# A planner's cost table, a split of each visit's last products, and three transfers in flight instead of five, in a retention + PReLU MLP kernel

## The chip, the cores and the metric

One core of a Trainium2 chip runs the whole program. The metric is device time in microseconds; lower is better. A measurement of this kernel tells about 0.3% from no change.

## The reference

Two stages in float32. The first is a retention layer: for each of 8 batches and 8 heads, `scores = q k^T / 8` over 576 positions of 64 numbers, multiplied by a lower triangle of decays `gamma_h ** (i - j)`, then times `v`. The result is turned to 4608 tokens by 512 channels. The second is an MLP:

```
h = x @ w_in                                   # 4608x512 by 512x2048
g = np.maximum(h, 0.0) + alpha * np.minimum(h, 0.0)
out = g @ w_out                                # 4608x2048 by 2048x512
```

## The kernel before, in words

**The MLP.** The tokens are cut into 18 blocks of 256, d_ff into 8 units of 256. A *cell* is one block with one unit: its first product (L1057, 48 matmuls of 256 columns in two halves) goes to the PSUM banks psh0 and psh1, ACT and DVE turn it into `ga` (L1064 to L1071), ACT and POOL split it into three pieces `g` (L1080 to L1087), and its second product (L1105, 12 matmuls of 512 columns, six for each half m of the tokens) adds to four banks pso. Both operands are split in pieces of a short float type ("fp32r"), so that three cheap products replace a slow float32 one. A *visit* is a block with four units (or all eight); at its end `evacuate` (L1116 to L1133) combines, for each m, two banks: first the bank p1 of the cross products (a subtraction on DVE, L1123, or a copy on ACT), then p0 (DVE, L1128), and a DMA takes the result to HBM. The first eight cells are done in plain float32 while weights are still being prepared (`unit_plain` L992, `second_plain` L1023).

**Retention.** Batches 0 and 1 are done early in parts (`load_part`, `part_transposes` L447, `part_scale` L423 on POOL, `part_scores` L471, `part_states` L493, `part_values` L540 and L556, `last_part`). Batches 2 to 7 are 24 pairs of heads, each one call of `joint` among the MLP cells: float32 matmuls of 64 columns that make scores and states ("su", L867 and L870, with two more matmuls "x", L860) of one pair and the values of the pair before ("v0" and "v1", L808, in the banks psh that the first products use too).

**The order.** Nothing is issued while this is described: `do` records each piece of work with an engine, a cost in us, a function, and what it reads and writes. `plan` first walks backwards for a due time of each piece, then forwards: at each step, on each engine, it takes the pieces that could begin within SLACK of the earliest one, and of these the one due first. SWITCH is added to a piece's earliest start if its *kind* differs from the last piece on that engine. The costs only choose the order of issue; on the chip each engine runs its own list in order, held up by semaphores. Before the change SLACK is 0.14 us and SWITCH 0.12 us on PE; only "su" pieces have a kind of their own ("half"), so the planner sees no difference between a value product and an MLP product.

**Transfers.** Nearly all DMAs are issued by one queue, SP's, in order (L220); the first two loads of q are issued by ACT. While the planned time is below LIMITED (100 us), a DMA on SP gets one more wait: going back over the DMAs planned before it, it adds their bytes to its own, and where the sum has reached IN_FLIGHT, it waits for the landing of the next older one. With 5 << 18 bytes that is the fifth DMA back for loads of 256 KiB. What stands behind a waiting DMA on SP waits too. In order, the early loads are: q, k of the first half of the first part, the same of the second half, v twice, four loads of w_in, two of w_out of 512 KiB, then the next parts and weights.

Of the kernel before, what the change touches and what calls it, by code (L numbers as in the profile page):

```python
# [21 lines left out]
def kernel(  # L22
# [58 lines left out]
    def piece(x):  # L81
        return x.bitcast(PIECE)
# [148 lines left out]
        do(eng, 0.56, f, r, w, late=size / rate, hold=hold)  # L231

    flight, now = [], [0.0]
    LIMITED, IN_FLIGHT = 100.0, 5 << 18

    LAT = {"PE": 0.2}

# [100 lines left out]
    BACKLOG, HOLD = 2.0, 30.0  # L338
    LAG, HOLD_X = 2, 100.0
    GROUPS = (("v0",), ("v1",), ("x", "su"))  # L340
    SLACK, SWITCH = {"PE": 0.14}, {"PE": 0.12}
    BEGIN = {"PE": 5.0, "ACT": 0.5, "DVE": 8.2, "POOL": 5.8, "SP": 0.5}


# [488 lines left out]
    def on_pe(parts, groups):  # L833
        for some in groups:
            do("PE", sum(parts[x][0] for x in some), lambda some=some: [parts[x][1]() for x in some],
               [key for x in some for key in parts[x][2]],
               [key for x in some for key in parts[x][3]],
               kind="half" if "su" in some else None)

    def joint(n):  # L840
        pv = [Gen(psh[m]) for m in range(2)]
        parts = {}
        if n - 1 in mts:
            (parts["v0"], parts["v1"]), rest = values(n - 1, pv)
        if n == len(pairs):
            on_pe(parts, [["v0"], ["v1"]])
            rest()
            return
        c = pairs[n][1]
        kT, qT = turned[n]  # L850
        kn, vn = loaded[n][2:]

        ss, uu = (Gen(x) for x in psa)

        def chunks(x):
            return x.get().rearrange("p (j s) -> p j s", s=C)

        def f():
            for h2 in range(2):
                nc.tensor.matmul(pv[1].get()[half(h2), 7 * C:], kT.get()[half(h2), chunk(NJ - 1)],  # L860
                                 qT.get()[half(h2), chunk(NJ - 1)], start=True, stop=True)
        parts["x"] = 0.067, f, [(kT, 0), (qT, 0)], [(pv[1], "x")]

        def f():
            for j in range(NJ - 1):
                for h2 in range(2):
                    nc.tensor.matmul(chunks(ss)[half(h2), j], kT.get()[half(h2), chunk(j)],  # L867
                                     qT.get()[half(h2), chunk(j)], start=True, stop=True,
                                     skip_group_check=True)
                    nc.tensor.matmul(chunks(uu)[half(h2), j], kn.get()[half(1 - h2), j],  # L870
                                     vns[n % 2][half(1 - h2), h2, j], start=True, stop=True,
                                     skip_group_check=True)
        parts["su"] = (1.05, f, [(kT, 0), (qT, 0), (kn, 0), (kn, 1), (vn, "v", 0), (vn, "v", 1)],
                       [(ss, 0), (uu, 0), (uu, 1)])
        on_pe(parts, [some for some in ([x for x in group if x in parts] for group in GROUPS)
                      if some])
        if n - 1 in mts:
            rest()
            if n + 1 < len(pairs):
                load_v(n + 1)  # L880
        mt = mts[n] = Gen(ats)
        for h2 in range(2):
            to = lambda h2=h2: mt.get()[half(h2), h2].rearrange("p j s -> p (j s)")
            dma(to, lambda h2=h2: qT.get()[half(h2)], S * D * 4, [(qT, 0)], [(mt, "q", h2)])

        def masked(h2, j, fro):
            x, h = half(h2), 2 * c + h2
            nc.vector.scalar_tensor_tensor(  # L888
                out=mt.get()[half(1 - h2), h2, j], in0=fro[x], scalar=pf[x, 1, h:h + 1],
                in1=mask[x, None, :].to_broadcast([C, fro.shape[1], C]), op0=ALU.mult,  # L890
                op1=ALU.mult)
        for h2 in range(2):
            do("DVE", 0.69, lambda h2=h2: masked(h2, slice(0, NJ - 1), chunks(ss)), [(ss, 0)],
               [(mt, "s", h2)])
        for h2 in range(2):
            do("DVE", 0.285, lambda h2=h2: masked(h2, slice(NJ - 1, NJ), chunks(pv[1])[:, 7:]),
               [(pv[1], "x")], [(mt, "x", h2)])
        su = Gen(sus)
        g1, g2 = gch[:, 0, c:c + 1], gch[:, 1, c:c + 1]
        do("ACT", 0.37, lambda: nc.scalar.copy(su.get()[:, 0::2], chunks(uu)[:, 0::2]), [(uu, 0)],  # L900
           [(su, "e")])
        do("DVE", 0.45, lambda: nc.vector.scalar_tensor_tensor(
            out=chunks(uu)[:, 1::2], in0=su.get()[:, 0::2], scalar=g1, in1=chunks(uu)[:, 1::2],
            op0=ALU.mult, op1=ALU.add), [(su, "e")], [(uu, 1)])
        do("ACT", 0.22, lambda: nc.scalar.copy(su.get()[:, 1], chunks(uu)[:, 1]), [(uu, 1)],
           [(su, 1)])
        for j in range(3, NJ - 1, 2):
            do("DVE", 0.285, lambda j=j: nc.vector.scalar_tensor_tensor(
                out=su.get()[:, j], in0=su.get()[:, j - 2], scalar=g2, in1=chunks(uu)[:, j],
                op0=ALU.mult, op1=ALU.add), [(su, j - 2), (uu, 1)], [(su, j)])  # L910
        do("DVE", 0.42, lambda: nc.vector.scalar_tensor_tensor(
            out=su.get()[:, 2::2], in0=su.get()[:, 1:NJ - 3:2], scalar=g1,
            in1=chunks(uu)[:, 2::2], op0=ALU.mult, op1=ALU.add),
            [(su, 1), (su, 3), (su, 5), (uu, 0)], [(su, "e")])
        for h2 in range(2):
            to = lambda h2=h2: vns[n % 2][half(h2), h2, 1:]
            keys = [(su, x) for x in ("e", 1, 3, 5, 7)]
            dma(to, lambda h2=h2: su.get()[half(h2)], (S - C) * D * 4, keys, [(vn, "s", h2)])
# [123 lines left out]
    def unit(cell):  # L1042
# [3 lines left out]
        for f in range(2):  # L1046
            ph = Gen(psh[f])

            def at(b, ph=ph):
                return ph.get()[:, b * TB:(b + 1) * TB]  # L1050

            def mm(f=f, at=at):
                for n, (b, l) in enumerate(((0, 0), (1, 2), (0, 1))):
                    for cc in range(NCC):
                        w = w_piece(u, cc // 2, l)
                        c0 = (cc % 2 * 2 + f) * P
                        nc.tensor.matmul(at(b), w[:, c0:c0 + P],  # L1057
                                         piece(x.get()[:, l, cc]), start=(n == 0 and cc == 0),
                                         stop=(n > 0 and cc == NCC - 1), skip_group_check=True)
            do("PE", 1.43, mm, [(x, l, n) for l in range(3) for n in range(2)] +  # L1060
               [w_at[u, i][l] for i in range(2) for l in range(3)], [(ph, 0), (ph, 1)])
            fc = 2 * u + f
            g = lambda f=f: ga.get()[:, f]
            do("ACT", 0.36, lambda g=g, at=at: nc.scalar.copy(g(), at(1)), [(ph, 1)], [(ga, f)])  # L1064
            do("DVE", 0.42, lambda g=g, at=at: nc.vector.scalar_tensor_tensor(  # L1065
                out=g(), in0=at(0), scalar=ONE, in1=g(), op0=ALU.mult, op1=ALU.subtract),
                [(ph, 0)], [(ga, f)])
            do("ACT", 0.39, lambda g=g, at=at: nc.scalar.activation(at(1), g(), ACTF.Relu,  # L1068
                                                                    scale=-1.0),
               [(ga, f)], [(ph, 1)])  # L1070
            do("DVE", 0.48, lambda g=g, at=at, fc=fc: nc.vector.scalar_tensor_tensor(  # L1071
                out=g(), in0=at(1), scalar=malpha[:, fc:fc + 1], in1=g(), op0=ALU.mult,
                op1=ALU.add), [(ph, 1), (cst, "a")], [(ga, f)])
# [19 lines left out]
    def second(cell):  # L1093
# [5 lines left out]
                dma(lambda: vis["o"].get(), lambda: o_kept[vis["kb"]], P * 4096,  # L1099
                    [(okm[vis["kb"]], 0), (okm[vis["kb"]], 1)], [(vis["o"], 0), (vis["o"], 1)])  # L1100
        for m in range(2):
            def mm(m=m, a=list(acc)):
                for f in range(2):
                    for b, l in ((0, 0), (0, 1), (1, 2)):
                        nc.tensor.matmul(a[2 * m + b].get(),  # L1105
                                         piece(g.get()[:, l, f, m * P:(m + 1) * P]),
                                         w_piece(u, 2 + f, l),
                                         start=(cell["first"] and f == 0 and l != 1),
                                         stop=(cell["last"] and f == 1 and l > 0))
            do("PE", 1.375, mm, [(g, l) for l in range(3)] +  # L1110
               [w_at[u, i][l] for i in (2, 3) for l in range(3)],
               [(acc[2 * m], 0), (acc[2 * m + 1], 0)])
            if cell["last"]:
                evacuate(vis, m)

# [248 lines left out]
```

## Time and profile before

| | |
|---|---|
| median of 3 runs | 954.3 us (952.51 to 955.4) |
| the profiled execution | 958.57 us |
| its span, first to last instruction | 956.5 us |
| around the span (difference) | 2.07 us |
| PE busy / DVE / ACT / POOL | 930.8 / 554.1 / 573.8 / 576.8 us |
| mean granted TensorE clock | 0.994 |
| DMA bytes | 121.05 MB, mean 127 GB/s |

PE is TensorE's matmuls, PEld its weight loads, DVE is VectorE, ACT ScalarE, POOL GpSimd, SP the queue engine. A row of the waits tells who waited for whom; a row of a timeline begins with its start and its length in us. In a timeline the lengths of neighbouring groups on PE overlap, since matmuls are pipelined, so a group's cost is read from its start to the start of the next.

### The profile page before, as it was taken

The page shows a single profiled execution, that of the slowest core. Times are in us where ns is not written, and L with a number is a line of the kernel's source. Part 1 is how long each engine was busy: PE and PEld are TensorE (multiplying, and loading weights), DVE is VectorE, ACT ScalarE, POOL GpSimd, SP SyncE. Part 2 cuts the span into 40 slices and gives each one's busy share as a digit, 9 for nine tenths or more (in the row PEclk, how much of TensorE's full clock was granted, in tenths as well). Part 3 has the DMA queues.
Part 4 walks back from the last instruction along what each step waited for, and adds up shares of the span by engine and source line. Part 5 has one row for each costly group of instructions (what it writes and reads, how often), then busy time and mean ns, then how long its engine had stood idle before and what let it go on. Part 6 is the DMA issues. An engine that isn't in the chain of part 4 may idle for free.

```text
span 956.5 us, 22974 instructions
## 1 busy us (share of the span) xinstructions
PE 930.8 (97%) x9009; PEld 820.8 (86%) x9009; DVE 554.1 (58%) x1180; ACT 573.8 (60%) x1285; POOL 576.8 (60%) x473
## 2 busy tenths in 40 slices
PE   4899999999999999999999999999999999999998
PEld 4666689888988898888999999999999999999996
DVE  5668566665766676766665754544444554444444
ACT  3446556657667666657876775555555555555542
POOL 3557765748865668745775565555555555555543
PEclk9899999999999999999999999999999999999999
DMA  8867587777877877785434411122222111121212
GB/s 213 203 178 149 134 182 170 151 173 166 186 181 179 199 178 171 209 174 147 155 121 144 156 54 45 67 78 78 86 88 70 67 67 66 66 67 68 66 45 66
DMA packets 235532, 121.05 MB, mean 127 GB/s; under 512 B 203408, under 2 KB 203424, under 8 KB 235424
## 3 DMA queue, kind: packets, MB, share of 16 engines
q1 hardware_dynamic: 233312, 119.05, 47.4%
q8 instruction: 71, 1.16, 0.5%
q10 hardware_dynamic: 2112, 0.53, 0.3%
q14 instruction: 37, 0.30, 0.1%
HBM read 74.19 MB, written 31.98 MB: 111 GB/s over the span
## 4 chain that ended last, share of the span: by engine, by line
PE 91%; DVE 2%; POOL 2%; ACT 2%; issue 1%; DMA 1%; ACTq 0%; POOLq 0%; DVEq 0%
PE psh L1057 40%; PE pso L1105 39%; PE psh L808 3%; PE pso L1023 2%; PE psh L992 2%; PE psa L870 2%; DMA w<-in_q_dram 1%; PE psh L860 1%; PE psa L867 1%; POOL w L732 1%; ACT x L571 1%; DVE psa L679 0%; POOL w L423 0%; ACT w L669 0%; POOL lx L975 0%
## 5 line engine op out<-in xcount | busy, mean ns | idle before, releaser
L1057 PEld LDWEIGHTS psh<-lx,w 128*128 128x128 f32 x2832 | 356.3, 191 | 11.6 <-DVE ga L1071 0.6
L1057 PE MATMUL psh<-lx,w 128*128 128x256 f32 x2832 | 364.2, 284 | 0.0
L1105 PE MATMUL pso<-w,g 128*128 128x512 f32 x1416 | 350.0, 393 | 1.4 <-DVE o L1128 1.2
L1084 POOL TENSOR_TENSOR g<-ga,g 128x512 fp32r<-128x512 f32 x136 | 175.8, 1293 | 243.4 <-ACT g L1080 217.8
L1105 PEld LDWEIGHTS pso<-w,g 128*128 128x128 f32 x1416 | 256.5, 189 | 50.0 <-DVE o L1128 1.4
L1065 DVE SCALAR_TENSOR_TENSOR ga<-psh,ga 128x256 f32<-128x256 f32 x272 | 115.0, 423 | 192.8 <-ACT ga L1064 189.3
L1087 POOL TENSOR_TENSOR g<-g 128x512 fp32r<-128x512 f32 x136 | 176.0, 1294 | 11.7 <-ACT g L1082 1.5
L1064 ACT COPY ga<-psh 128x256 f32<-128x256 f32 x272 | 101.3, 373 | 134.7 <-PE psh L1057 118.4
L1071 DVE SCALAR_TENSOR_TENSOR ga<-psh,malpha,ga 128x256 f32<-128x256 f32 x272 | 130.7, 481 | 69.5 <-ACT psh L1068 68.6
L1068 ACT ACTIVATE psh<-ga 128x256 f32<-128x256 f32 x272 | 105.6, 388 | 82.1 <-DVE ga L1065 81.8
L1080 ACT ACTIVATE g<-ga 128x512 fp32r<-128x512 f32 x136 | 85.7, 630 | 55.9 <-DVE ga L1071 52.1
L975 POOL TENSOR_TENSOR lx<-lx 128x512 fp32r<-128x512 f32 x66 | 84.7, 1295 | 44.4 <-DVE lx L965 36.2
L1082 ACT ACTIVATE g<-ga 128x512 fp32r<-128x512 f32 x136 | 84.4, 620 | 0.0
L888 DVE SCALAR_TENSOR_TENSOR at<-psa,pf,mask 64x512 f32<-64x512 f32 x48 | 36.0, 750 | 31.6 <-PE psa L867 29.0
L958 ACT ACTIVATE lx<-x 128x512 fp32r<-128x512 f32 x66 | 41.2, 627 | 0.0
L808 PEld LDWEIGHTS psh<-at,vn 128*64 128x64 f32 x864 | 27.9, 137 | 10.8 <-issue 6.8
L972 POOL TENSOR_TENSOR lx<-x,lx 128x512 fp32r<-128x512 f32 x24 | 31.0, 1294 | 5.0 <-DVE wa L681 2.1
L693 POOL TENSOR_TENSOR wa<-wa,op 128x512 int32<-128x512 int32 x16 | 21.0, 1311 | 21.5 <-DVE wa L690 11.7
L808 PE MATMUL psh<-at,vn 128*64 128x64 f32 x864 | 32.6, 226 | 1.1 <-DVE ga L1071 1.1
L1123 DVE TENSOR_TENSOR op<-pso,op 128x512 f32<-128x512 f32 x34 | 23.3, 687 | 15.3 <-PE pso L1105 15.3
L965 DVE TENSOR_TENSOR lx<-x,psa 128x512 fp32r<-128x512 f32 x42 | 28.5, 679 | 2.7 <-PE psh L1057 2.1
L827 ACT COPY x<-psh 128x256 f32<-128x256 f32 (+3 forms) x72 | 20.7, 321 | 15.3 <-PE psh L808 11.7
(210 smaller groups left out, 1114.4 us busy)
## 6 DMA issues: line engine op xcount, KB each, us to landing
xk<-x SPq DMA_DIRECT2D x18, 512.0 KB, 4.2
out_dram<-o SPq DMA_DIRECT2D x36, 256.0 KB, 2.3
ok<-o SPq DMA_DIRECT2D x34, 256.0 KB, 3.2
x<-xk SPq DMA_DIRECT2D x17, 512.0 KB, 4.9
op<-ok SPq DMA_DIRECT2D x17, 512.0 KB, 4.0
qx<-in_q_dram SPq DMA_DIRECT2D x96, 72.0 KB, 3.1
kx<-in_k_dram SPq DMA_DIRECT2D x96, 72.0 KB, 2.7
kn<-in_k_dram SPq DMA_DIRECT2D x48, 144.0 KB, 3.2
```

The lines of the kernel that those rows point to most:

```text
L808: nc.tensor.matmul(pv[i].get()[half(h2), (j - js[0]) * C:(j - js[0] + 1) * C], vns[n % 2][:, h2, j], mt.get()[:, h2, j], start=True, stop= ...
L975: do("POOL", 1.29, lambda c=c: nc.gpsimd.tensor_tensor(out=piece(to.get()[:, 2, c]), in0=to.get()[:, 0, c], in1=to.get()[:, 1, c], op=ALU. ...
L1057: nc.tensor.matmul(at(b), w[:, c0:c0 + P], piece(x.get()[:, l, cc]), start=(n == 0 and cc == 0), stop=(n > 0 and cc == NCC - 1), skip_grou ...
L1064: do("ACT", 0.36, lambda g=g, at=at: nc.scalar.copy(g(), at(1)), [(ph, 1)], [(ga, f)])
L1065: do("DVE", 0.42, lambda g=g, at=at: nc.vector.scalar_tensor_tensor(out=g(), in0=at(0), scalar=ONE, in1=g(), op0=ALU.mult, op1=ALU.subtrac ...
L1068: do("ACT", 0.39, lambda g=g, at=at: nc.scalar.activation(at(1), g(), ACTF.Relu, scale=-1.0), [(ga, f)], [(ph, 1)])
L1071: do("DVE", 0.48, lambda g=g, at=at, fc=fc: nc.vector.scalar_tensor_tensor(out=g(), in0=at(1), scalar=malpha[:, fc:fc + 1], in1=g(), op0=A ...
L1080: do("ACT", 0.64, lambda: nc.scalar.mul(piece(to.get()[:, 2]), ga.get(), BELOW), both, [(to, 2)])
L1082: do("ACT", 0.64, lambda: nc.scalar.mul(piece(to.get()[:, 0]), ga.get(), BELOW * 2.0 ** -12), both, [(to, 0)])
L1084: do("POOL", 1.29, lambda: nc.gpsimd.tensor_tensor(out=piece(to.get()[:, 1]), in0=ga.get(), in1=to.get()[:, 2], op=ALU.subtract), both + [ ...
L1087: do("POOL", 1.29, lambda: nc.gpsimd.tensor_tensor(out=piece(to.get()[:, 2]), in0=to.get()[:, 0], in1=to.get()[:, 1], op=ALU.subtract), [( ...
L1105: nc.tensor.matmul(a[2 * m + b].get(), piece(g.get()[:, l, f, m * P:(m + 1) * P]), w_piece(u, 2 + f, l), start=(cell["first"] and f == 0 a ...
```

## The change

IN_FLIGHT falls from 5 to 3 times 256 KiB. The kind "half" goes; the split products of both MLP layers get a kind "pieces", so that a switch between them and all other PE work counts, at 0.1 us, with a SLACK of 0.3 us. Five planned costs move. In the last cell of each visit the second product of each m becomes two pieces: first the two matmuls of the cross bank p1, then the four of p0, where it was one piece of six in the order p0, p0, p1 twice.

```diff
-    LIMITED, IN_FLIGHT = 100.0, 5 << 18
+    LIMITED, IN_FLIGHT = 100.0, 3 << 18
...
-    SLACK, SWITCH = {"PE": 0.14}, {"PE": 0.12}
+    SLACK, SWITCH = {"PE": 0.3}, {"PE": 0.1}
...
-               [key for x in some for key in parts[x][3]],
-               kind="half" if "su" in some else None)
+               [key for x in some for key in parts[x][3]])
...
-        parts["x"] = 0.067, f, [(kT, 0), (qT, 0)], [(pv[1], "x")]
+        parts["x"] = 0.02, f, [(kT, 0), (qT, 0)], [(pv[1], "x")]
...
-        parts["su"] = (1.05, f, [(kT, 0), (qT, 0), (kn, 0), (kn, 1), (vn, "v", 0), (vn, "v", 1)],
+        parts["su"] = (1.09, f, [(kT, 0), (qT, 0), (kn, 0), (kn, 1), (vn, "v", 0), (vn, "v", 1)],
...
-            do("DVE", 0.69, lambda h2=h2: masked(h2, slice(0, NJ - 1), chunks(ss)), [(ss, 0)],
+            do("DVE", 0.75, lambda h2=h2: masked(h2, slice(0, NJ - 1), chunks(ss)), [(ss, 0)],
...
-        do("DVE", 0.45, lambda: nc.vector.scalar_tensor_tensor(
+        do("DVE", 0.485, lambda: nc.vector.scalar_tensor_tensor(
...
-               [w_at[u, i][l] for i in range(2) for l in range(3)], [(ph, 0), (ph, 1)])
+               [w_at[u, i][l] for i in range(2) for l in range(3)], [(ph, 0), (ph, 1)], kind="pieces")
...
-            def mm(m=m, a=list(acc)):
-                for f in range(2):
-                    for b, l in ((0, 0), (0, 1), (1, 2)):
...
-            do("PE", 1.375, mm, [(g, l) for l in range(3)] +
-               [w_at[u, i][l] for i in (2, 3) for l in range(3)],
-               [(acc[2 * m], 0), (acc[2 * m + 1], 0)])
+            terms = ((0, 0), (0, 1)), ((1, 2),)
+            for some in reversed(terms) if cell["last"] else (sum(terms, ()),):
+                def mm(m=m, a=list(acc), some=some):
+                    for f in range(2):
+                        for b, l in some:
...
+                do("PE", 0.459 * len(some), mm, [(g, l) for _, l in some] +
+                   [w_at[u, i][l] for i in (2, 3) for _, l in some],
+                   [(acc[2 * m + b], 0) for b in sorted({b for b, _ in some})], kind="pieces")
```

More of the change, by code (lines that the diff above doesn't have):

```diff
@@ L1101, in second @@
         for m in range(2):
-            def mm(m=m, a=list(acc)):
-                for f in range(2):
-                    for b, l in ((0, 0), (0, 1), (1, 2)):
[L1105 to L1109, printed above, removed]
-            do("PE", 1.375, mm, [(g, l) for l in range(3)] +
-               [w_at[u, i][l] for i in (2, 3) for l in range(3)],
-               [(acc[2 * m], 0), (acc[2 * m + 1], 0)])
+            terms = ((0, 0), (0, 1)), ((1, 2),)
[3 more added lines that the diff above has]
+                        for b, l in some:
+                            nc.tensor.matmul(a[2 * m + b].get(),
+                                             piece(g.get()[:, l, f, m * P:(m + 1) * P]),
+                                             w_piece(u, 2 + f, l),
+                                             start=(cell["first"] and f == 0 and l != 1),
+                                             stop=(cell["last"] and f == 1 and l > 0))
+                do("PE", 0.459 * len(some), mm, [(g, l) for _, l in some] +
+                   [w_at[u, i][l] for i in (2, 3) for _, l in some],
+                   [(acc[2 * m + b], 0) for b in sorted({b for b, _ in some})], kind="pieces")
             if cell["last"]:
```

## The prediction

> **What bounds the kernel now.** First the busy times in three stages, cut where the retention pairs begin and end on PE.
>
> ```profile
> core 0: us, PE busy (x) PEld busy (x) DVE busy (x) ACT busy (x) POOL busy (x), PEclk, DMA share, GB/s
> 0.00:100.00 100.00, 81.27 (x1507) 60.35 (x1508) 65.47 (x142) 48.86 (x88) 57.73 (x66) 0.95 0.77 181
> 100.00:466.00 366.00, 363.45 (x4408) 317.99 (x4407) 241.99 (x538) 236.74 (x562) 239.53 (x191) 1.00 0.73 173
> 466.00:957.00 491.00, 486.09 (x3098) 442.50 (x3096) 246.62 (x500) 288.21 (x636) 279.50 (x218) 1.00 0.24 80
> ```
>
> After 100 us PE is full but for 2.6 us and a tail of 4.9, and no other engine passes two thirds. There only PE's own work, its few waits and the tail can be shortened. In the first 100 us PE idles 18.7 us, and the loads run at 181 GB/s. Who makes PE wait comes second, the first three rows from the first 26 us, the others after 100 us:
>
> ```profile
> PE psa L447 <- DMA w<-in_k_dram: 4.3, 1, 4.3
> PE pso L447 <- POOL w L423: 3.6, 2, 2.8
> PE pso L556 <- issue: 3.2, 1, 3.2
> ...
> PE pso L1105 <- DVE o L1128: 1.2, 1, 1.2
> PE psh L808 <- DVE ga L1071: 1.1, 3, 0.6
> PE pso L1105 <- POOL g L1087: 0.3, 1, 0.3
> ```
>
> POOL L423 in row two waits for q; its timeline:
>
> ```profile
> 7.00 1.05 POOL L423 TENSOR_TENSOR w<-w,tp 128x512 f32<-128x512 f32 x1 [3.90 <-DMA w<-in_q_dram]
> 8.99 3.04 POOL L423 TENSOR_TENSOR w<-w,tp 128x512 f32<-128x512 f32 x3 [0.94 <-DMA w<-in_q_dram]
> ```
>
> The third view is two-microsecond windows around the "issue" row, a stop that no semaphore explains (PE stands from 17.26 to 20.45), with two rows of the chain of waits, start and length ahead: the same 16 plain first products early, and later at full clock.
>
> ```profile
> 16.00:18.00 2.00, 1.26 (x69) 1.03 (x63) 1.83 (x5) 0.00 (x0) 0.00 (x0) 1.00 1.06 260
> 18.00:20.00 2.00, 0.00 (x0) 0.00 (x0) 1.84 (x3) 0.00 (x0) 0.69 (x1) 0.89 0.18 36
> 20.00:22.00 2.00, 1.55 (x78) 1.55 (x81) 1.39 (x2) 0.24 (x1) 1.02 (x2) 0.50 0.76 171
> ...
> 23.74 6.71 PE psh L992 x16
> 106.90 3.65 PE psh L992 x16
> ```
>
> At 18 to 20 us the DMA engines are nearly still too (36 GB/s) though loads are pending. The granted clock is then 0.50 until about 29.6, and the same products take 6.71 us, not 3.65.
>
> **The early loads.** Byte counts and PE's early order stay; each engine's list is the same up to about 110 us. What is new is that SP waits for the third load back. Queued behind each such wait is every later load on SP; who waits for those are POOL L423, PE L447 and the weight preparation (ACT, DVE, POOL). At the start k's second half now waits for q's first half. In the trace SP sends both halves of k at once: q's first half, issued at 1.29, lands at 6.83, k's halves at 4.13 and 6.35. Without the second k ahead, its 256 KiB (about 1.1 us at the 230 to 250 GB/s of these first us) drop out of q's way: q near 5.5 and 6.8, not 6.83 and 8.86. k's second half, issued at 5.5, lands 3.3 us later (as v's second half does, 6.85 to 10.18), at 8.8. POOL scales q to 7.9, PE turns q to 8.9 and k to 9.9: the scores begin at about 10.0, not 12.0, and the chain of DVE and POOL behind them moves as much. That is -2.0 us if it is kept. Later loads land 1 to 2 us later by such counting (two w_out blocks near 18 and 20 us, before 15.9 and 20.1), where their readers come several us after landing.
>
> [...] The stage to 47 us moves 9.91 MB at 211. [...]
>
> The stop at 17.26 is undecided: nothing in the trace names it but still DMAs beside it. I keep it. [...]
>
> **Order of issue after 100 us.** I counted in both orders of issue. Matmuls are the same in number. Switches between the split products and the others fall from 67 to 57; value products cut in two by a second product from 8 to 4 pairs. Their price, from PE's timeline:
>
> ```profile
> 185.85 3.04 PE L1057 MATMUL psh<-lx,w 128*128 128x256 f32 x24
> 188.72 1.55 PE L1105 MATMUL pso<-w,g 128*128 128x512 f32 x6
> 190.20 0.80 PE L808 MATMUL psh<-at,vn 128*64 128x64 f32 x20
> 190.93 1.66 PE L1105 MATMUL pso<-w,g 128*128 128x512 f32 x6
> 192.52 0.69 PE L808 MATMUL psh<-at,vn 128*64 128x64 f32 x16
> 193.14 0.27 PE L860 MATMUL psh<-qT,kT 64*64 64x64 f32 x2
> ```
>
> From start to start the six take 1.48 us before values and 1.59 between them; between split products they take 1.39 elsewhere. That is 0.1 per switch. The two value halves take 0.73 + 0.62 = 1.35; whole they take 1.20 elsewhere: 0.15 per cut. So -10 x 0.1 - 4 x 0.15 = -1.6 us. As a check, the whole order from 112 us at undisturbed prices with these and the 2.6 us of waits makes 839.6 us; the trace has 839.8.
>
> The waits: in the new order values follow a first product within 1.5 us 6 times, before 11, and that is where they waited for DVE L1071; the bank p1 is let go earlier, which is what L1128 held. New ones could come, as SP's retention loads and copies are reordered too, and ACT, DVE and POOL with them. But PE waited for no DMA there, and the smallest distance from a pair's states to its values stays at 9.7 us of PE work against some 3 us for a copy to land; from a first to its second product it stays at 5.2. I take -0.8 for the waits, between -2.6 (all go) and +3 (more than double).
>
> The five planned costs change no instruction; what they do to the order is in these counts. The split of the last second product adds no matmul.
>
> **The tail.** At the end, with the last matmul near 952.1:
>
> ```profile
> 950.77 0.69 DVE L1123 TENSOR_TENSOR op<-pso,op 128x512 f32<-128x512 f32 x1 [6.42 <-PE pso L1105]
> 951.49 0.69 DVE L1128 SCALAR_TENSOR_TENSOR o<-pso,op 128x512 f32<-128x512 f32 x1
> 952.12 0.69 DVE L1123 TENSOR_TENSOR op<-pso,op 128x512 f32<-128x512 f32 x1
> 952.85 0.69 DVE L1128 SCALAR_TENSOR_TENSOR o<-pso,op 128x512 f32<-128x512 f32 x1
> ```
>
> Now p1 is complete four matmuls (4 x 0.23 = 0.92 us) before p0, so L1123 runs under them and only L1128 follows the last matmul. That removes 0.7 us; next is L1128 and the output's DMA, which stay.
>
> **Sum.** Early -2.0, order -1.6, waits -0.8, tail -0.7: -5.1 us. Against the profiled execution 958.6 - 5.1 = 953.5; that execution lies 4.3 us above the median of 954.3, and I take the sum from the median: 949.2.
>
> **Rivals.** (1) Three under way also end the stop: -3.2 and -3.1 more, of which the loads may hold back some 2: 944.9. For it: the DMA engines stood still just when most was pending, and three pending clog less. Against: PE's burst of small matmuls before it stays as it is, and in unprofiled runs the stop may be missing anyway. (2) The loads starve, slower: a landing gets no shorter with fewer under way. The loaded stage shows medians of 4.3 to 5.9 us for 256 KiB; at 4.7 us three give 167 GB/s, and 9.91 MB take 59 us, 12 later. The preparation of weights before L992 and L1023 has some 5 us of slack, so about 7 us reach PE: 954.3 + 7 - 3.1 = 958.2. It decides from the point where landings stay above about 3.9 us (786 KB over 3.9 us is below 200 GB/s). Against: deep queues make those landings long. (3) The new order makes PE wait: the waits reach 5 us and eat the order's gain: with -2.0 early lost again on the way to 100 us, 954.3 - 1.6 + 2.4 - 0.7 = 954.4. (4) The limit does nothing: q lands as before or its gain is waited away: 951.2.
>
> **Chances.** My sum 0.36, (1) 0.20, (4) 0.15, (3) 0.16, (2) 0.13. A measurement tells 0.3%, 2.9 us. Faster: my sum, (1) and half of (4), whose 951.2 is at the border of 951.4: 0.62; within: half of (4) and (3): 0.25; slower 0.13. The range leaves out (2) and the outer part of (1): 943.5 to 956.5.
>
> **What would show it.** POOL's first L423 at about 5.7 and the scores near 10; k's second half landing near 8.8; mean rate to 47 us still over 200 GB/s; the "issue" row and the clock of 0.50 at 20 to 28 us kept; PE's idle time after 100 us below 2 us and first products after scores no rarer than 19; the last L1123 begun before PE's last matmul ends. Wrong it would be if PE waits for POOL lx L693 or for DMAs more than now before 100 us, if new rows of over 1 us stand in the waits after it, or if the stop is gone.

## The result and the profile after

| | before | after |
|---|---|---|
| median | 955.32 us (10 runs, 952.51 to 958.3) | 950.04 us (10 runs, 948.57 to 952.77) |
| the profiled execution | 958.57 us | 950.54 us |
| its span | 956.5 us | 948.8 us |
| mean granted clock in it | 0.994 | 0.995 |

The ratio of the times is 0.9951, 95% interval 0.9936 to 0.9967: 4.7 us less. The forecast of 949.2 us and the time agree; two of its four terms do not.

The busy times of the changed kernel in the stages of before (columns: window, its length, busy us and count of PE, PEld, DVE, ACT, POOL, then granted clock, DMA share, GB/s):

```profile
core 0: us, PE busy (x) PEld busy (x) DVE busy (x) ACT busy (x) POOL busy (x), PEclk, DMA share, GB/s
0.00:100.00 100.00, 83.11 (x1532) 60.64 (x1533) 67.26 (x146) 52.17 (x94) 60.31 (x68) 0.97 0.79 183
100.00:466.00 366.00, 365.36 (x4429) 322.56 (x4428) 244.15 (x545) 237.52 (x570) 243.79 (x194) 1.00 0.74 178
466.00:957.00 491.00, 477.98 (x3050) 435.33 (x3049) 239.48 (x492) 282.75 (x623) 272.48 (x212) 1.00 0.23 76
```

PE is busy 8.1 us less in the last stage, since its last matmul ends 8.1 us earlier (943.98 for 952.09), and in the middle it idles 0.6 us, where it idled 2.6. The early stage still has 16.9 us of idle time. Who makes PE wait in the changed kernel, first the four longest rows of its first 26 us, then, after the dots, the only row after 100 us:

```profile
PE psa L447 <- DMA w<-in_k_dram: 4.3, 1, 4.3
PE psh L991 <- ACT x L571: 1.8, 1, 1.8
PE pso L556 <- issue: 1.4, 1, 1.4
PE pso L447 <- POOL w L423: 1.2, 1, 1.2
...
PE psh L808 <- DVE ga L1070: 0.5, 1, 0.5
```

The wait for POOL L423 shrank from 3.6 us to 1.2 as forecast, and of three rows after 100 us one is left. Grown is the second row: the plain first products (L991, before L992) wait for the copies of x, here 1.8 us, and 2.5 more between 26 and 100 us; before they waited 1.1 in all. POOL's timeline in the changed kernel holds the early gain:

```profile
5.53 2.04 POOL L423 TENSOR_TENSOR w<-w,tp 128x512 f32<-128x512 f32 x2 [2.43 <-DVE tp L141]
9.89 2.04 POOL L423 TENSOR_TENSOR w<-w,tp 128x512 f32<-128x512 f32 x2 [2.31 <-DMA w<-in_v_dram]
```

q is there at 5.36 and 6.33 us, k's second half lands at 8.55, the scores begin at 9.64 and no longer at 11.99. The windows around the old stop, in the changed kernel:

```profile
16.00:18.00 2.00, 1.07 (x78) 0.88 (x58) 1.58 (x3) 1.99 (x4) 1.29 (x1) 0.92 0.81 236
18.00:20.00 2.00, 1.10 (x3) 0.95 (x4) 1.61 (x4) 1.97 (x4) 1.15 (x1) 0.50 0.91 259
20.00:22.00 2.00, 2.00 (x6) 1.57 (x5) 1.65 (x4) 0.80 (x3) 0.95 (x3) 0.50 0.68 156
```

No window is empty on PE any more, and the DMA engines go on; but PE is busy only 2.17 of the 4 us from 16 to 20, and the granted clock is 0.50 from 17.70 to 24.52 us all the same. The tail, DVE's last four instructions, with PE's last matmul ending at 943.98:

```profile
941.75 0.69 DVE L1125 TENSOR_TENSOR op<-pso,op 128x512 f32<-128x512 f32 x1 [5.51 <-PE pso L1107]
942.66 0.69 DVE L1130 SCALAR_TENSOR_TENSOR o<-pso,op 128x512 f32<-128x512 f32 x1 [0.22 <-PE pso L1107]
943.27 0.68 DVE L1125 TENSOR_TENSOR op<-pso,op 128x512 f32<-128x512 f32 x1
944.05 0.69 DVE L1130 SCALAR_TENSOR_TENSOR o<-pso,op 128x512 f32<-128x512 f32 x1
```

The last subtraction lies under PE's last matmuls; only L1130 follows.

**A mark that separates the stages.** PE's list after the first "su" is fixed once planned, and loads no longer hold it up. So the stretch from the first "su" to the end of PE's last matmul shows the planner's part alone, and the time of the first "su" the loads' part. Before: 112.19 to 952.09, 839.90 us. After: 109.03 to 943.98, 834.95. The order took 4.95 us out, the tail 0.7 (from 1.45 to 0.76 us between last matmul and last DVE instruction). That alone makes 5.6 us, more than the whole result, so in the runs the early part must have brought nothing, although in these two profiled executions its first "su" comes 3.2 us sooner. The experiments take the parts one by one.

### The profile page after: what moved, and what is told of

Same layout as the page of the kernel before. It is cut to its first block, busy times and chain, and to the rows that moved or that the text cites. A ratio compares the mean times of both kernels' runs of the same rounds, so it can differ in the third digit from the quotient of the medians.

```text
span 948.8 us, 22949 instructions
## 1 busy us (share of the span) xinstructions
PE 926.4 (98%) x9009; PEld 818.5 (86%) x9009; DVE 550.9 (58%) x1180; ACT 572.4 (60%) x1285; POOL 576.6 (61%) x473
## 4 chain that ended last, share of the span: by engine, by line
PE 88%; DMA 7%; SPq 2%; DVE 1%; ACT 1%; issue 1%; POOL 0%; ACTq 0%; DVEq 0%
PE psh L1056 41%; PE pso L1107 39%; PE psh L808 3%; PE psa L869 2%; DMA w<-in_moe_w_out_dram 2%; SPq L220 2%; DMA w<-in_v_dram 2%; DMA w<-in_k_dram 1%; PE psh L991 1%; PE pso L1022 1%; DMA lx<-in_moe_w_in_dram 1%; DMA w<-in_q_dram 1%; DMA w<-in_moe_w_in_dram 1%; PE psh L859 1%; PE psa L866 1%
## 5 line engine op out<-in xcount | busy, mean ns | idle before, releaser
L808 PEld LDWEIGHTS psh<-at,vn 128*64 128x64 f32 x864 | 27.5, 138 | 9.0 <-issue 6.4
L780 POOL TENSOR_TENSOR qx<-qx,tabx 128x576 f32<-128x576 f32 x24 | 27.6, 1148 | 11.2 <-DVE wa L690 3.9
L808 PE MATMUL psh<-at,vn 128*64 128x64 f32 x864 | 31.4, 225 | 0.5 <-DVE ga L1070 0.5
L991 PE MATMUL psh<-x,lx 128*128 128x256 f32 x96 | 25.4, 418 | 4.7 <-POOL lx L693 1.8
L1056 PE MATMUL psh<-lx,kT 128*128 128x256 f32 x144 | 29.0, 283 | 0.0
```

Of the source, the lines that this page charges most:

```text
L808: nc.tensor.matmul(pv[i].get()[half(h2), (j - js[0]) * C:(j - js[0] + 1) * C], vns[n % 2][:, h2, j], mt.get()[:, h2, j], start=True, stop= ...
L1056: nc.tensor.matmul(at(b), w[:, c0:c0 + P], piece(x.get()[:, l, cc]), start=(n == 0 and cc == 0), stop=(n > 0 and cc == NCC - 1), skip_grou ...
```

## The experiments

Each ratio is to the kernel before, with the 95% interval. "Su to end" is the stretch just defined. "Clock" is the time that the half clock can have cost, worked out as (1 - mean granted clock over all runs of the kernel) x time; it is an upper value for the recorded half clock, since PE also stands in part of that time, and since half clock after the last matmul counts in it too (1.4 us in the changed kernel's profiled execution). The record of the clock begins with its first change, at 16.16 us in the kernel before and at 10.87 in the changed one, and what lies ahead of that is not in the column.

| kernel | median us | ratio | first "su" us | su to end us | clock us |
|---|---|---|---|---|---|
| the changed kernel, second time | 950.0 | 0.9952 [0.9937, 0.9968] | 108.61 | 834.95 | 4.4 |
| planner and split only | 948.62 | 0.9944 [0.9924, 0.9963] | 107.57 | 834.89 | 2.1 |
| three under way only | 954.04 | 0.9991 [0.9977, 1.0005] | 107.52 | 839.87 | 3.6 |
| changed, no split | 951.97 | 0.9971 [0.9959, 0.9982] | 109.25 | 836.27 | 4.3 |
| changed, three at the start only | 946.36 | 0.9911 [0.9893, 0.9929] | 104.71 | 834.92 | 1.9 |
| changed, three up to load 42 | 949.15 | 0.9939 [0.9927, 0.9951] | 106.81 | 834.95 | 3.6 |
| changed, three at the start and from load 42 | 945.62 | 0.9905 [0.9890, 0.9919] | 104.37 | 834.99 | 1.3 |
| changed, no limit after the start | 949.81 | 0.9941 [0.9927, 0.9955] | 109.48 | 835.45 | 4.6 |
| changed, three up to load 13 | 946.98 | 0.9924 [0.9911, 0.9936] | 105.98 | 834.93 | 3.0 |
| changed, three at the start and from 13 to 42 | 946.26 | 0.9918 [0.9901, 0.9934] | 108.34 | 834.97 | 2.5 |
| before, three at the start only | 950.69 | 0.9960 [0.9948, 0.9972] | 104.36 | 839.82 | 1.1 |
| before, split only | 951.08 | 0.9969 [0.9956, 0.9981] | 105.91 | 837.67 | 1.7 |

The kernel before, run beside them, had medians of 954.4, 954.75 and 954.6 us and a clock column of 2.4, 2.6 and 1.7. The first "su" is from one profiled execution each and carries that execution's own half clocks; the ratios decide.

**The parts apart.** The changed kernel with five under way:

```diff
-    LIMITED, IN_FLIGHT = 100.0, 3 << 18
+    LIMITED, IN_FLIGHT = 100.0, 5 << 18
```

> The changed kernel with five transfers under way again; PE's order is that of the change (57 switches). Theory A (the early gain comes from three under way: q lands at 5.4 and not 6.8, and the stop of PE near 15 us shrinks): only order, waits and tail are left, so about 3.0 us below the kernel before (ratio 0.997), q at POOL near 7.0 again, and PE's stop with it. Rival B (the planner's changes carry all of the gain, three under way is nothing on the clock): about 5 us below (ratio 0.9945). Rival C (three under way costs later what it gains): below 0.9945.

And the kernel before with three:

```diff
-    LIMITED, IN_FLIGHT = 100.0, 5 << 18
+    LIMITED, IN_FLIGHT = 100.0, 3 << 18
```

> The kernel before with three under way and nothing else; PE's order is that of before (67 switches). Theory A: about 2 us below the kernel before (0.998), POOL's first scaling near 5.5 us, retention beginning on PE some 3 us earlier in the profile. Rival B: no difference (1.000). Rival C: slower, 1.002 or more.

The first gave 0.9944 and the second 0.9991. The planner and the split are the whole gain; three under way throughout is worth nothing that a measurement can tell, on the old order or on the new. Yet its scores begin at 9.64, the full 2.4 us earlier. A start that is kept and a time that isn't: so something later gives it back. One more expectation failed: with five under way I awaited a long "issue" stop, and it was 0.8 us.

**The start without the later limit.** In the changed kernel the first six loads (q, k, v) keep three, all later ones get five:

```diff
-                    if eng == "SP" and ahead >= IN_FLIGHT:
+                    if eng == "SP" and ahead >= (IN_FLIGHT if len(flight) > 5 else 3 << 18):
...
-    LIMITED, IN_FLIGHT = 100.0, 3 << 18
+    LIMITED, IN_FLIGHT = 100.0, 5 << 18
```

> The changed kernel with three under way only for k's second half and v's two halves, five for all later loads. Theory A1 (the early gain is q's landing alone, and the later limit only delays weight loads, as the late w_out load at 77 us that gave some 2 us back): faster than the changed kernel by up to 2 us, ratio to before 0.993. Theory A2 (the later limit is what shortens the stop of PE near 15 us and lets it start earlier): slower than the changed kernel by 1 to 3 us, with a stop of 3 us back in the profile.

It gave 0.9911: by the ratios 3.9 us below the changed kernel (0.9952) and 3.2 below five throughout (0.9944; by the medians 2.3). Its interval lies clear of the changed kernel's and just touches that of five throughout; but all its six runs, at most 946.92 us, are below all eight with five, at least 947.88. So three at the start gain, and three later lose about as much. The rates of the first 47 us, the changed kernel first:

```profile
0.00:47.00 47.00, 34.37 (x714) 26.45 (x715) 31.16 (x83) 20.47 (x34) 24.63 (x36) 0.93 0.83 194
```

and with three at the start only:

```profile
0.00:47.00 47.00, 35.31 (x731) 26.47 (x733) 31.57 (x84) 20.52 (x34) 27.61 (x39) 0.96 0.98 228
```

228 GB/s became 194. One place where it reaches PE is seen in ACT's timeline, the changed kernel first (start, length, operation, in brackets the idle time before and who ended it):

```profile
12.78 0.68 ACT L669 ACTIVATE kT<-lx 128x512 f32<-128x512 f32 x1 [2.44 <-DMA lx<-in_moe_w_in_dram]
...
15.85 0.69 ACT L669 ACTIVATE qT<-lx 128x512 f32<-128x512 f32 x1 [1.81 <-DMA lx<-in_moe_w_in_dram]
...
17.01 1.75 ACT L571 COPY x<-pso 128x512 f32<-128x512 f32 x3
```

the same three rows with three at the start only:

```profile
12.23 0.68 ACT L669 ACTIVATE kT<-lx 128x512 f32<-128x512 f32 x1 [2.11 <-DMA lx<-in_moe_w_in_dram]
...
13.61 0.68 ACT L669 ACTIVATE qT<-lx 128x512 f32<-128x512 f32 x1
...
15.80 1.77 ACT L571 COPY x<-pso 128x512 f32<-128x512 f32 x3 [0.98 <-PE pso L556]
```

In the second ACT is early and waits for PE before the copies; in the first it waits 1.81 us for the last block of w_in, and the copies stand behind it in ACT's list. So a late weight holds up a copy that PE needs sooner. But PE itself was late too with the products that are copied, again the changed kernel first:

```profile
15.71 1.21 PE L556 MATMUL pso<-g,w 64*32 64x64 f32 x82 [1.38 <-issue]
14.97 1.21 PE L556 MATMUL pso<-g,w 64*32 64x64 f32 x82 [0.86 <-issue]
```

From this start to the copies it is 1.30 us in the first and 0.83 in the second. Of the 1.21 us between 15.80 and 17.01, PE's later start is thus 0.74 and the wait for w_in 0.47.

PE's starts in the two traces show the rest. In the changed kernel the first plain products (L991) begin 1.2 us later, and what follows them 2.4 us later, since at half clock for longer they take 6.3 us and not 5.1 (the granted clock is 0.50 from 20 to 24 us in the one; in the other 0.78 from 20 to 22 and 1.00 from 22 to 24). Up to 76 us nothing more is added. Then ACT waits for a late weight again, 1.93 us for a block of w_out at 77.28, and PE at 93.77 has waited 2.5 us for copies of x, where it waits 1.4 in the other. At the first "su" the difference is 4.3 us.

**Which of the later loads.** Three up to load 42 and then five; three at the start, five for loads 6 to 41 and three again after; and no limit after the start:

```diff
-                    if eng == "SP" and ahead >= IN_FLIGHT:
+                    if eng == "SP" and ahead >= (IN_FLIGHT if len(flight) < 42 else 5 << 18):
```

> The changed kernel with three under way for the first 42 loads and five after. The limit on the later loads costs some 3.3 us (changed kernel near 949.7 against 946.4 with three at the start alone). Theory D (the loads are behind all along to 55 us: PE's marks are 1.1 us later by its first plain product and 1.2 to 2.1 at 50 us): most of the loss stays, ratio to before 0.994, about 949. Theory E (it is the w_out blocks at 70 to 77 us and the loads after them): the loss goes, ratio near 0.991.

```diff
-                    if eng == "SP" and ahead >= IN_FLIGHT:
+                    if eng == "SP" and ahead >= (5 << 18 if 6 <= len(flight) < 42 else IN_FLIGHT):
```

> The complement: three under way for k's second half and v's halves, five to the 42nd load, three again after it. Theory D: little loss, ratio near 0.992. Theory E: the whole loss, ratio near 0.9945. If the ratios of this and of its complement lie in the middle (0.993), both stretches cost.

```diff
-                    if eng == "SP" and ahead >= IN_FLIGHT:
+                    if eng == "SP" and ahead >= (IN_FLIGHT if len(flight) < 6 else 99 << 18):
```

> Three under way for k's second half and v's halves, then no limit by bytes at all. [...] If deep queues make landings long, as my prediction held against starving: slower, 0.993 or more, with a longer stop of PE near 15 us.

and the changed kernel itself beside them:

> The changed kernel itself, as the measure for the other three on the same chip: ratio 0.995, as first measured. If three at the start alone is really 3 us faster than it and this is no matter of chips, it stays above 0.994.

They gave 0.9939, 0.9905, 0.9941 and 0.9952. The loss arises between loads 6 and 41; from load 42 on three cost nothing where five stood before it (where three did, five from there on gave 0.9939 for 0.9952, within the intervals). Three at the start and from load 42 is the fastest kernel of all, 9.1 us below the kernel before. Without any limit the loads are no faster (227 GB/s to 47 us) and the time is about 2.9 us worse than with five (0.9941 to 0.9911; the intervals just touch). In its trace PE's "issue" stop is 2.5 us, where it is 0.9 with five for the later loads, and SP has a long row:

```profile
10.42 2.49 SPq L220 DMA_DIRECT2D w<-in_k_dram  x2
12.95 5.19 SPq L220 DMA_DIRECT2D w<-in_q_dram  x2
18.18 3.22 SPq L220 DMA_DIRECT2D w<-in_moe_w_in_dram  x4
```

To issue two loads of q took SP 5.19 us, where four of w_in take 3.22. But the same two took 4.65 us in the kernel before, with five under way, so the missing limit is not shown to be what holds SP.

**The two stretches of the loss.** Three up to load 13 and then five, and three at the start and from 13 to 41:

```diff
-                    if eng == "SP" and ahead >= IN_FLIGHT:
+                    if eng == "SP" and ahead >= (IN_FLIGHT if len(flight) < 13 else 5 << 18):
```

> The changed kernel with three under way for the first 13 loads (to the two w_out blocks), five after. Theory F (the loss is that ACT, in order, waits for the third and fourth w_in blocks at 15.8 us, and its copies of x, for which PE's first plain product waits, stand behind it): most of the 2.7 us between three to the 42nd load (0.9939) and three at the start alone (0.9911) shows here, ratio near 0.9935, with ACT's second w_in wait of about 1.8 us and its copies of x beginning near 17 us, not 15.8. Rival (the loss is later): ratio near 0.991.

```diff
-                    if eng == "SP" and ahead >= IN_FLIGHT:
+                    if eng == "SP" and ahead >= (IN_FLIGHT if len(flight) < 6 or 13 <= len(flight) < 42 else 5 << 18):
```

> Three under way for k's second half and v's halves, five for the four w_in and two w_out blocks, three from there to the 42nd load, five after. Theory F: near three at the start alone, ratio 0.9915, ACT's copies of x at 15.8 us. Rival: near 0.9935.

They gave 0.9924 and 0.9918, against 0.9911 for neither and 0.9939 for both. With three up to load 13 ACT waited 1.95 us for w_in and the copies began at 16.76, near the 17.01 of the changed kernel (0.9 us of it by that wait, worked out as above), but only 1.2 us of the 2.7 came of it; the second stretch alone cost 0.7. The intervals of these two overlap with each other and with 0.9911, so the shares are rough: neither stretch carries the loss alone.

**The start, and the split, on the old order.** The kernel before with three for the first six loads only:

```diff
-                    if eng == "SP" and ahead >= IN_FLIGHT:
+                    if eng == "SP" and ahead >= (IN_FLIGHT if len(flight) > 5 else 3 << 18):
```

> The kernel before with three under way for k's second half and v's halves alone, five after. If start and order are independent: the 2.2 to 3.3 us that this is worth on the changed kernel, ratio 0.9970, about 952; retention begins on PE near 105 us and takes 839.9 us to the last matmul as in the kernel before. If the start's gain is not kept here: 0.999 as with three throughout.

It gave 0.9960, 3.8 us: the start's gain is there without the planner changes. Then the changed kernel without the split of the last second products:

```diff
-            for some in reversed(terms) if cell["last"] else (sum(terms, ()),):
+            for some in (sum(terms, ()),):
```

> The changed kernel without the split of each visit's last second product (one piece of six matmuls again); the planner then makes 61 switches and 6 pairs of cut values, not 57 and 4. Theory A: 0.7 us of tail, 4 x 0.1 + 2 x 0.15 = 0.7 us of order and part of the waits come back: 1.5 to 2.5 us above the changed kernel, ratio to the kernel before near 0.997, and in its profile only 0.7 us more from the last matmul to the last DVE end. Rival (the split is worth its tail alone): 0.7 us above the changed kernel.

and the kernel before with the split alone:

```diff
-            def mm(m=m, a=list(acc)):
-                for f in range(2):
-                    for b, l in ((0, 0), (0, 1), (1, 2)):
...
+            terms = ((0, 0), (0, 1)), ((1, 2),)
+            for some in reversed(terms) if cell["last"] else (sum(terms, ()),):
+                def mm(m=m, a=list(acc), some=some):
+                    for f in range(2):
+                        for b, l in some:
...
```

> The kernel before with only the split of each visit's last second product; its order then has 63 switches and 7 cut pairs. Theory: 0.7 us of tail, 0.4 + 0.15 us of order, and the wait for DVE L1128 (1.5 us from start to start) goes because the cross bank is let go earlier: 2.5 us in all, ratio 0.9974. Rival: the tail alone, 0.9993.

They gave 0.9971 and 0.9969. Without the split the changed kernel loses 1.8 us: 1.3 between "su" and the end, 0.7 in the tail. The split alone brings 3.0 us to the old order: 2.2 in the order, 0.7 in the tail. The two gains overlap, since either shortens the same waits. With the split alone these are left after 110 us:

```profile
PE pso L1107 <- DVE o L1130: 0.8, 1, 0.8
PE psh L808 <- DVE ga L1071: 0.3, 1, 0.3
PE pso L1107 <- POOL g L1087: 0.3, 1, 0.3
```

of 1.2, 1.1 and 0.3 before: the bank p1 is let go sooner, but the next block's products still come to it too early. The changed kernel without the split has no wait on that bank at all, and only L808 waits, twice, 0.7 us in all. So it is the new order that ends this wait, with the split or without.

## Why the prediction came out right

The sum, -5.1 us, was met by -4.7; two of its four terms were wrong by 2 us or more, with opposite signs. That they cancel is luck.

**Order: -1.6 forecast, -1.5 found.** I took the start-to-start time of every piece on PE after the first "su" and subtracted what its kind takes undisturbed. The small excesses, at switches and cuts, sum to 8.46 us before and 6.94 after. That fits the prices of 0.1 per switch and 0.15 per cut, though no run takes the two apart. (A cell's first product is 24 matmuls, as in the row "L1057 x24", and not the 48 of the description.)

**Waits: -0.8 forecast, -3.4 found.** This is a term that was mis-sized. The rows of idle time sum to 2.6 us before, and I took a third of them. In the start-to-start times the same five stalls cost 4.2 us (1.47 us the largest, on the bank p1), and one is left, of 0.78. A row of idle time counts only PE standing still; from start to start it costs 1.6 us more over the five. Four of the five stalls went. Most of that is the new order, which has values within 1.5 us of a first product 6 times and not 11: with it and without the split, 0.7 us of idle rows are left. The third rival, that the new order makes PE wait, falls: su to end is 834.9 to 835.0 us in eight of the nine profiled kernels with the whole new order, whatever their loads, and 835.45 in the one without a limit.

**Tail: -0.7 forecast, -0.7 found**, between the last matmul and the last DVE instruction. Without the split it is 1.45 us again.

**Early: -2.0 forecast, about 0 found.** The failed step is to let the later loads cost nothing since "their readers come several us after landing". The marks of the start came as forecast (POOL at 5.53 for 5.7, scores at 9.64 for 10.0, k's second half at 8.55 for 8.8), and the start was worth more than 2.0: 3.2 us on the new order, 3.8 on the old. But the rate to 47 us didn't stay over 200 GB/s; it fell to 194, from 211 before and 228 with the better start and five. That it would stay was my estimate from one landing of before: three loads, 786 KB, in the 3.3 us from 6.85 to 10.18, which is 238 GB/s. I let it stand for a stage of 47 us, of which in the changed kernel the windows from 14 to 24 us alone run from 156 to 259. And I looked for the loads' readers but missed the list that they stand in: ACT waits for w_in, and later for w_out, with the copies of x behind it. Two slips change nothing: the chances of "faster" and "within" add to 0.635 and 0.235, not 0.62 and 0.25, and 786 KB over 3.9 us is 202 GB/s, not below 200.

Part of the loss comes by the clock. The clock column parts the kernels: where three hold from load 6 to 41, it shows 3.6 to 4.4 us (4.8 over the changed kernel's first ten runs), with five there 1.1 to 2.6, with the two mixtures 2.5 and 3.0, without a limit 4.6. Between the changed kernel and its version with three at the start only (4.4 and 1.9) that is up to 2.5 of the 3.9 us; the rest are longer waits. It fits the profiled executions: the granted clock is 0.50 for 6.83 us in the changed kernel; with three at the start it is 0.87, 0.50 and 0.78 in the three windows from 16 to 22 us, which makes 3.4 us at 0.50. What sets it is not shown; no run here changes PE's idle time alone.

**The rivals.** The second, starving loads, was right in direction, 3.9 us, and I gave it 0.13 as it also had to outweigh the start, which it only matched. Its ground, that a landing gets no shorter with fewer under way, held for two of five groups only: from 7 to 47 us, with five and with three, the median from issue to landing of 256 KiB is 6.4 and 5.0 us for k, 6.1 and 3.8 for q, 5.0 and 3.1 for the later w_in, but 4.1 and 4.4 for v, 3.4 and 4.0 for the first four of w_in. And three loads of 256 KiB at 194 GB/s still mean 4.05 us (an estimate), above the 3.9 at which it was to decide. The fourth had two ways. "Q lands as before" fails in the trace, where the scores move by 2.4 us; "its gain is waited away" is what happened (0.9991 alone), and its 951.2 us lies as near to the 950.0 found as my 949.2. The first, that the stop goes, came half: it shrank from 3.2 us to 1.4, and the half clock lasted 6.83 us, not 10.24, in the profiled executions. But the stop was 0.8 us with five under way and the new planner, so three don't set it. This rival's further 3.1 us (6.71 - 3.65) took the half clock to go with the stop, an estimate that no run shows; in the runs they went apart, with a stop of 0.8 us and a clock of 1.00 from 14 to 24 us (the split alone), and with a stop of 0.9 and a clock of 0.50 from 18 to 20 (three at the start only). The profiled execution of before had drawn a long half clock: its mean of 0.994 stands against 0.9975 over 25 runs of that kernel, and its 958.57 us against their median of 954.4. The step "I take the sum from the median" kept that out of the time, but I described it as the kernel's usual course.

I wrote of the stop that "nothing in the trace names it". The records of the DMA engines have one thing more beside it. Both profiles have this row (queue and kind, then packets, MB and share):

```profile
q8 instruction: 71, 1.16, 0.5%
```

These are blocks of 16 KiB. Before, the first of them came from 17.96 to 18.85 us and PE went on at 20.45; in the changed kernel, from 13.25 to 14.18 and at 15.71. So the stop ends 1.6 and 1.5 us after the block has landed, both times before the same matmul of L556. That PE waits for the block is my estimate from these two pairs of times; no run here isolates it, nor what makes the block come late by so much or so little.

## What to carry to other kernels

Here the limit on transfers under way had two effects: with three in place of five q's first half landed at 5.36 us and no longer at 6.83, and the rate to 47 us was 194 GB/s, where five after the same start gave 228. One number for both is a compromise: where one load is urgent and the next is not, keep the queue short; where many loads are wanted soon, keep it deep enough for the rate, here five of 256 KiB (946.36 us) and not three (950.0), and not without limit (949.81). When costing later landings, look not only at the reader of the load but at all that its engine holds behind it in order. A right sum can hide two errors, so run the parts apart: here three at the start, five for loads 6 to 41 gave 945.62 us, 0.9905 of the time before, against 0.9952 for the change.

## What the runs showed of the hardware

In the profiled executions the granted clock was 0.50 for 10.24 us in the kernel before (19.57 to 29.82) and for 6.83 in the changed one (17.70 to 24.52); with the split alone it was 1.00 from 14 to 24 us. How much half clock there is differs from run to run of one kernel: the mean clock over ten runs of the changed kernel spans 0.994 to 0.998, and the version with three at the start and from 13 to 41 ran from 944.86 us at 0.999 to 949.88 at 0.993.

PE was partly busy ahead of the half clock. The last 3.41 us at full clock, in the kernel before and in the changed one:

```profile
16.16:19.57 3.41, 1.10 (x62) 0.87 (x57) 3.12 (x6) 0.00 (x0) 0.26 (x1) 1.00 0.68 161
14.28:17.70 3.42, 1.41 (x86) 1.17 (x82) 2.93 (x5) 1.84 (x4) 1.29 (x1) 1.00 0.69 205
```

PE was busy 1.10 and 1.41 us of them. By windows of two microseconds it was busy 1.76 of the 4 us from 14 to 18 with three at the start only and 1.53 without a limit, and the clock was 0.50 from 18 to 20 in the first and from 20 to 24 in the second. With the split alone it was busy 1.80 of the 4 us from 16 to 20, and the clock stayed at 1.00. So half clock followed in four of these five executions and not in the fifth; no run shows what decides.

PE was slow ahead of the record's first change too: in the changed kernel its first scores come every 26.6 ns up to 10.87 us, and later ones, from 31.14 us, every 15.0. In the kernel before that first change comes at 16.16 us, and all the first scores, from 11.99 to 13.66, come every 26.6 ns.

The stop in L556 that no semaphore explains is 3.2 us long in the kernel before, 1.4 in the changed one, 2.5 without a limit and 0.6 with three up to load 13. In the first two it ends 1.6 and 1.5 us after a 16 KiB block of kind "instruction" has landed.

q's first half, issued by ACT at 1.29 us in both kernels, landed at 6.83 us where SP had sent both halves of k beside it, and at 5.36 where it had sent one.
